# Forty-seven turns of the identity tile into unread PSUM tiles in the opening of a chunk-select attention and gated FFN kernel

## The chip, the cores and the metric

The kernel runs on one core of a Trainium2 chip. The metric is the device time of one execution in microseconds. Four compute engines work beside each other: TensorE (PE in the profile; its weight loads are PEld), VectorE (DVE), ScalarE (ACT) and GpSimd (POOL). SyncE (SP) issues most of the DMA transfers, GpSimd the ones for the weights. Each engine takes its instructions in the order of its own queue and waits for the others by semaphores.

## The reference

Attention over selected chunks comes first, for 4 batches, 8 heads, 768 positions and a head size of 64, and then a gated FFN over its 3072 rows of 512.

```python
k_chunks = k.reshape(B, H, nc, 32, D)                      # 24 chunks of 32 keys
k_min, k_max = k_chunks.min(3), k_chunks.max(3)
ub = sum over d of max(q * k_min, q * k_max)               # an upper bound per query and chunk
ub = where(chunk of the query >= chunk, ub, -1e9)
sel = the 6 chunks with the highest ub, per query
scores = where(sel and causal, q @ k.T / 8, -1e9)
x = softmax(scores) @ v                                    # -> [3072, 512]
out = (sigmoid(x @ w_gate) * (x @ w_val)) @ w_out          # d_ff = 1536
```

## The kernel before

The 3072 rows are cut into eight units of 384 rows (three blocks of 128). Unit 0 holds the first blocks of batches 0, 1 and 2, whose queries see fewer than six chunks, so nothing is selected for them; these blocks go through their own short path (`first`, L590). The other units take the remaining blocks in order. For each unit the kernel brings keys and queries into the layout with the head dimension on the partitions, works out the bounds and the selection (`choose`), attends, and runs the FFN. Units 4 to 7 run their FFN in pairs with sums of weights prepared beforehand.

Every operation is first written down as an entry of a plan (`Plan.add`, L50) with a name, the engines that it can run on, what it reads and what it writes. The durations that stand in the entries are not read when the kernel is built. The order of all operations is a list written out by hand, the string `ORDER` (L95): each word is an operation's name, behind `@` its engine if it isn't the first of its entry, and behind `:` the slots of the buffers that it is the first to use. PSUM tiles (`ps`) have eight slots, one per bank. `Plan.order` (L79) goes through the words, and each engine's queue holds its operations in that order. A tile that takes a slot waits for the last reader of the tile that had it before.

The names that matter in the opening, all of them in the list's first lines:

- `ident` (L461): `make_identity` on GpSimd fills `ident32`, a 128x128 float32 identity; `ident16` is its float16 copy.
- `kf{e}_{b}`, `qf{e}_{b}`, `vf_{b}` (L516 to L530): SyncE loads the first blocks' keys, queries and values of batch b. `k{p}_u1`, `q{p}_u1` and the same for u2 (L532) load keys and queries for units 1 and 2; `v_0_1` to `v_0_5` (L556) load the other value blocks of batch 0.
- `kfT_b`, `qfT_b` (L600): four float32 turns each on TensorE (`nc.tensor.transpose` with `ident32`) of the first blocks; `kf16_b`, `qf16_b` cast the results to float16.
- `scf_b` (L637): eight score matmuls; `expf` (L642) the exponential; `cmf` (L644) the causal mask on GpSimd; `pvf` (L651) the product with the values; `rzf`, `xf` the division on VectorE; `xpsf` (L666) two float16 turns of the result, `xTf` its copy to SBUF.
- `kn`, `kT`, `qn`, `qT` (L675 to L688): for units 1 and 2, a copy of the raw block and then three or two float32 turns on TensorE.
- `after0`, `after1` (L496): two one-element copies on GpSimd that read a landed query tile. The weights' loads `wg`, `wv`, `wo` (L501 to L510), three of each on GpSimd's DMA queue, depend on them.
- `g_u0_*`, `v_u0_*` (L937): the FFN of unit 0, and `o*_u0_*` (L968) its output product; `pv_u1_*` (L881) unit 1's product with the values; `v16_0_*` (L564) GpSimd's casts of the value blocks.

TensorE's queue in the opening is: `qfT_1`, `kT_u1_1`, `kfT_0`, `qfT_0`, `scf_0`, `kfT_1`, `kfT_2`, `scf_1`, `qfT_2`, `pvf_0_0`, `pvf_0_1`, `xpsf_0_0`, `pvf_1_0`, `xpsf_0_1`, `scf_2`, `xpsf_1_0`, `pvf_2_0`, `kT_u1_0`, and so on up to `g_u0_0`.

Of the kernel before, what the change touches and what calls it, by code (L numbers as in the profile page):

```python
# [99 lines left out]
expf_0_1:3 q1_u1 pvf_0_0:6 qf16_2:4 after1 rzf_0_0:0 k1_u2:1 cmf_0_1 xf_0_0:0 kt_u1_1:0 q1_u2 cmf_1_0 vc_1@ACT  # L100
pvf_0_1:7 k2_u2 xpsf_0_0:0,0 v11 expf_1_1:1 pvf_1_0:5 k3_u2 vc_2 rzf_1_0:0 rzf_0_1:1 hq1 cmf_1_1 xf_0_1:1 hkp101 wg1
kxf0 q0_u2 kxf1:0 xpsf_0_1:4 scf_2:6,3,3 expf_2_0 qn_u1_0@POOL:1 kn_u1_2:5 expf_2_1:2 xf_1_0:2 cmf_2_0 ap1 kn_u1_0:2
wv1 kx1_u1_1:1 xpsf_1_0:7 pvf_2_0:6 xTf_0_0@ACT kT_u1_0:2 xTf_0_1 cmf_2_1 rzf_2_0:0 xf_2_0:0 k0_u2 pvf_1_1:5 wg2
kx1_u1_0 xpsf_2_0:3 qn_u1_3:4 pvf_2_1:0 hk1_u1_1@ACT rzf_2_1:0 wv2 qn_u1_2@DVE:2 wo1 v_0_3:5 xf_2_1:1 rzf_1_1:0
xTf_2_0 qT_u1_0:1 xf_1_1:2 kn_u1_3:6 wo0 xTf_1_0 kT_u1_2:4 hkp110@ACT kt_u1_0@DVE:1 kx0_u1_0 qT_u1_3:6 v_0_2:3
hkf0@ACT qn_u1_1@POOL:0 qf_u1_3:0 xpsf_1_1:0 qf_u1_0 xpsf_2_1:3 xTf_2_1 kT_u1_3:5 xTf_1_1 qT_u1_2:7 qf_u1_2@DVE
g_u0_0:2,0,0 kx0_u1_3 hq0_u1_2@POOL qT_u1_1:3 kcr_f v_u0_0:0 qm_u1_2@POOL:0 qf_u1_1@DVE qm_u1_0@ACT g_u0_1:7,1,1
kx1_u1_2 hq0_u1_0 qm_u1_3@POOL kx1_u1_3 tanh_u0_0 v_u0_1:6 qm_u1_1@POOL kt_u1_2@DVE:2 g_u0_2:1,2,2 kx0_u1_2
hk1_u1_2@ACT vf1_3:1 kcr1 kcr_u1@POOL hk0_u1_2@ACT hg_u0_0 v_u0_2:3 ub_u1:2,4 tanh_u0_2 hk0_u1_0 tanh_u0_1 hg_u0_2
# [5 lines left out]
sc_u1_3_1:2,0 v_u0_7:4 hk0_u2_2@POOL kT_u2_0:3 exp_u1_0_2 sc_u1_3_2:6 hq1_u1_2@POOL g_u0_8:1,3,8 hq0_u2_1@DVE
hk1_u1_3@ACT hk1_u1_0@POOL exp_u1_1_2 kx1_u2_2:0 v_u0_8:7 qn_u2_0:0 ap1_u1 exp_u1_3_2 kx0_u2_2 sc_u1_3_0:0 sc_u1_2_2:6
apt1_u1 exp_u1_3_0 sc_u1_2_1:5 hg_u0_7 kn_u2_3:5 kf0_3 qT_u2_0:0 cm_u1_3 hqm1_u1_2@DVE exp_u1_2_2 sc_u1_0_0:4 cm_u1_1
qf_u2_0 g_u0_9:6,2,9 exp_u1_3_1 tanh_u0_8 kT_u2_1:0 hq0_u2_0@POOL v_u0_9:2 hq1_u1_1 cm_u1_2 kx1_u2_1 hqm1_u1_0@ACT
hg_u0_8 g_u0_10:1,1,10 kx0_u2_0 v_u0_10:7 exp_u1_2_1 kx1_u2_0 tanh_u0_10 hk1_u2_2 kT_u2_3:5 exp_u1_0_0 hg_u0_10
g_u0_11:1,0,11 kx1_u2_3 cm_u1_0 sc_u1_0_1:4 kt_u2_3@DVE:0 v_u0_11:7 hkf1 exp_u1_0_1 kx0_u2_3 tanh_u0_9 v16_0_3  # L120
o0_u0_0:4,0 kt_u2_0:2 hg_u0_9 tanh_u0_11 hk1_u2_3@POOL hk1_u2_0 kt_u2_1:1 sc_u1_1_1:5 q2_u2 o1_u0_0 hg_u0_11
hk0_u2_1@ACT q3_u2 kx0_u2_1 exp_u1_1_1 k11_1:0 hq1_u1_0 qf1_3:2 v16_0_2 o2_u0_0 v16_0_1 hk0_u2_3@POOL pv_u1_2:6
osb_u0_0@DVE kfT_3:3 qn_u2_3:4 sc_u1_5_0:2,2 kcr_u2 qn_u2_2:2 pv_u1_1:1 kf16_3@DVE:0 qf0_3 pv_u1_0 qT_u2_3:7 out_u0_0
rz_u1_0:0 qT_u2_2:0 sc_u1_6_2:5,3 pv_u1_3 k01_1 qf_u2_2 sc_u1_7_0:4,0 exp_u1_5_0 rz_u1_1:1 o0_u0_1:3,1 vf_3:1 qm_u2_2
qf_u2_3@DVE hq0_u2_2 x_u1_0:0 exp_u1_6_2 sc_u1_7_2:0 sc_u1_4_2:2,1 x_u1_1:2 exp_u1_7_2 sc_u1_7_1:7 o1_u0_1 exp_u1_4_2
qm_u2_3 exp_u1_7_0 qm_u2_0 sc_u1_5_2:1 hq1_u2_1 sc_u1_6_0:5 cm_u1_7 exp_u1_7_1 sc_u1_5_1:0 cm_u1_5 exp_u1_5_1
sc_u1_4_0:6 ub_u2:2,4 k10_1 exp_u1_6_0 k00_1 exp_u1_5_2 xps_u1_0:7,1 exp_u1_4_0 sc_u1_6_1:0 ubn0_u2:0 sc_u1_4_1:5
qfT_3:1 xT_u1_0 exp_u1_4_1 cm_u1_4 mx0_u2:0 o2_u0_1 hk0_u2_0@ACT hq0_u2_3@POOL ubn1_u2 exp_u1_6_1 hq1_u2_3@POOL
pv_u1_5:2 qf16_3:6 mx1_u2 cm_u1_6 pv_u1_7:6 vc_3@ACT pv_u1_4 v_0_5:5 hq1_u2_0@DVE pv_u1_6 rz_u1_2:0 scf_3:7,5,0 ap1_u2
# [1235 lines left out]
```

## Time and profile before

| | |
|---|---|
| Median of three runs | 289.07 us (287.99 to 289.54) |
| The profiled execution | 286.49 us |
| Its span, first to last instruction | 284.5 us |
| TensorE busy | 265.6 us, 93% |
| VectorE busy | 248.8 us, 87% |
| ScalarE busy | 209.5 us, 74% |
| GpSimd busy | 162.1 us, 57% |
| DMA | 34.28 MB in 130035 packets |

How to read the rows below. Times count from the first instruction of the profiled execution. A row of the stretches gives for each engine the busy time and the number of instructions, then the granted clock, the mean busy share of the 16 DMA engines (over 1 where packets overlap) and the bytes moved per time. A row of the timeline gives start, duration, engine, source line, operation, tiles written and read, shape and count; in brackets stands how long the engine had been idle before and what ended that. A piece of the chain is a start, a duration and who worked; the chain follows what ended last back to its cause. A row of one tile gives the shortest, median and longest duration of one instruction. The duration of a matmul reaches to the arrival of its result, so matmuls that follow each other overlap: the pace is the distance between starts.

### The profile page before, as it was taken

The page shows a single profiled execution, that of the slowest core. Times are in us where ns is not written, and L with a number is a line of the kernel's source. Part 1 is how long each engine was busy: PE and PEld are TensorE (multiplying, and loading weights), DVE is VectorE, ACT ScalarE, POOL GpSimd, SP SyncE. Part 2 cuts the span into 40 slices and gives each one's busy share as a digit, 9 for nine tenths or more (in the row PEclk, how much of TensorE's full clock was granted, in tenths as well). Part 3 has the DMA queues.
Part 4 walks back from the last instruction along what each step waited for, and adds up shares of the span by engine and source line. Part 5 has one row for each costly group of instructions (what it writes and reads, how often), then busy time and mean ns, then how long its engine had stood idle before and what let it go on. Part 6 is the DMA issues. An engine that isn't in the chain of part 4 may idle for free.

```text
span 284.5 us, 7266 instructions
## 1 busy us (share of the span) xinstructions
PE 265.6 (93%) x2668; PEld 180.9 (64%) x2668; DVE 248.8 (87%) x660; ACT 209.5 (74%) x457; POOL 162.1 (57%) x231
## 2 busy tenths in 40 slices
PE   1859999799999999999999999999899999999994
PEld 1637565567764666664767756676476786765784
DVE  6569987569998998989979899999999989999972
ACT  2477579488779788668799997899899647758621
POOL 7298634246257559569776866357848700076720
PEclk9999999999999999999999999999999999999999
DMA  7999999999999999919335013030000211001005
GB/s 169 254 214 219 213 197 206 197 186 221 186 181 215 188 247 210 175 30 216 80 75 140 6 30 81 37 69 13 16 14 17 64 40 75 2 37 76 1 2 221
DMA packets 130035, 34.28 MB, mean 120 GB/s; under 512 B 118096, under 2 KB 127056, under 8 KB 130000
## 3 DMA queue, kind: packets, MB, share of 16 engines
q1 hardware_dynamic: 125248, 29.11, 48.5%
q0 software_dynamic: 4752, 4.72, 9.9%
q8 instruction: 21, 0.34, 0.5%
q14 instruction: 14, 0.11, 0.1%
HBM read 30.67 MB, written 6.29 MB: 130 GB/s over the span
## 4 chain that ended last, share of the span: by engine, by line
PE 66%; DVE 11%; DMA 9%; SPq 4%; ACT 3%; POOL 3%; issue 2%; DVEq 0%; POOLq 0%; ACTq 0%
PE sc_u L848 9%; PE o_u L968 9%; PE g_u L937 8%; PE v_u L937 8%; PE pv_u L881 5%; DMA kq_u<-in_k_dram 5%; DMA v<-in_v_dram 4%; PE suo_u6u L1195 3%; PE suo_u4u L1195 2%; PE ube_u L787 2%; PE suv_u6u L1054 2%; DVE hg_u L1084 2%; PE sug_u6u L1054 2%; DVE hgp_u L1084 2%; SPq L538 2%
## 5 line engine op out<-in xcount | busy, mean ns | idle before, releaser
L859 ACT ACTIVATE att_u<-sc_u 128x512 f16<-128x512 f32 (+3 forms) x184 | 92.1, 552 | 15.9 <-PE sc_u L848 14.4
L865 POOL TENSOR_SCALAR_AFFINE_SELECT att_u<-att_u 128x384 f16<-128x384 f16 (+1 forms) x56 | 30.7, 556 | 44.3 <-ACT att_u L859 35.5
L937 PE MATMUL g_u<-xT_u,wg 128*128 128x384 f16 x192 | 39.1, 326 | 0.1
L937 PE MATMUL v_u<-xT_u,wv 128*128 128x384 f16 x192 | 39.0, 326 | 0.1
L968 PE MATMUL o_u<-wo,hg_u 128*128 128x512 f16 x144 | 35.3, 379 | 1.0 <-DMA wo<-in_moe_w_out_dram 1.0
L949 DVE SCALAR_TENSOR_TENSOR hg_u<-gate_u,v_u 128x384 f16<-128x384 f16 x48 | 25.1, 535 | 4.3 <-PE v_u L937 2.4
L881 PEld LDWEIGHTS <-att_u 128*128 128x128 f16 x640 | 24.9, 98 | 5.5 <-issue 1.5
L881 PE MATMUL pv_u<-v,att_u 128*128 128x65 f16 x640 | 27.3, 193 | 1.1 <-POOL v L564 1.0
L945 ACT ACTIVATE gate_u<-g_u 128x384 f16<-128x384 f32 x48 | 23.3, 495 | 6.7 <-PE g_u L937 6.5
L848 PE MATMUL sc_u<-hqe,hke 128*128 128x128 f16 (+2 forms) x220 | 27.8, 243 | 0.1
L848 PE MATMUL sc_u<-hqo,hko 128*128 128x128 f16 (+2 forms) x220 | 27.3, 243 | 0.1
L937 PEld LDWEIGHTS <-wg 128*128 128x128 f16 x192 | 18.1, 98 | 10.4 <-issue 0.8
L937 PEld LDWEIGHTS <-wv 128*128 128x128 f16 x192 | 18.1, 98 | 10.5 <-DMA wv<-in_moe_w_val_dram 0.4
L968 PEld LDWEIGHTS <-hg_u 128*128 128x128 f16 x144 | 13.2, 98 | 13.7 <-DVE kcr L572 1.3
L848 PEld LDWEIGHTS <-hke 128*128 128x128 f16 x220 | 17.0, 98 | 7.3 <-issue 1.0
L848 PEld LDWEIGHTS <-hko 128*128 128x128 f16 x220 | 16.8, 98 | 6.4 <-issue 0.9
L1177 POOL TENSOR_TENSOR v<-v,hg_u 128x384 f16<-128x384 f16 x6 | 6.0, 996 | 24.1 <-PE sug_u6u L1054 22.3
L564 POOL CAST v<-v 128x512 f16<-128x512 f32 x23 | 14.8, 644 | 7.0 <-DMA v<-in_v_dram 5.8
L900 DVE TENSOR_TENSOR x_u<-pv_u,rz_u 128x384 f16<-128x384 f32 (+1 forms) x28 | 14.7, 529 | 0.6
L1054 PEld LDWEIGHTS <-Sg 128*128 128x128 f16 x96 | 9.1, 98 | 6.1 <-issue 1.4
L810 DVE MAX8 mx_u<-ubn_u 128x8 f32<-128x8 f32 (+16 forms) x152 | 12.5, 158 | 0.3
L1054 PEld LDWEIGHTS <-Sv 128*128 128x128 f16 x96 | 9.0, 98 | 5.4 <-issue 0.5
(280 smaller groups left out, 699.3 us busy)
## 6 DMA issues: line engine op xcount, KB each, us to landing
...
wg<-in_moe_w_gate_dram POOLq DMA_DIRECT2D x3, 512.0 KB, 11.5
wv<-in_moe_w_val_dram POOLq DMA_DIRECT2D x3, 512.0 KB, 12.8
wo<-in_moe_w_out_dram POOLq DMA_DIRECT2D x3, 512.0 KB, 20.3
...
```

Source lines behind the costliest of these rows:

```text
L564: plan.add(f"v16_{b}_{ib}", {POOL: pool(H * D)}, lambda e: nc.gpsimd.tensor_copy(v16[b % 2][:, ib, :, 0:D], at(t)), reads=[t], writes=[("v ...
L848: nc.tensor.matmul(at(t)[:, o:o + 128 * m], hk[b % 2][e_][:, p, 128 * jb:128 * jb + 128], hq[u.side][e_][:, p, 128 * x:128 * (x + m)], sta ...
L859: plan.add(f"exp_{u.name}_{h}_{y}", {ACT: act(n)}, lambda e, t=t, att=att, b0=b0, n=n: nc.scalar.activation(at(att)[:, b0:b0 + n], at(t), ...
L865: nc.gpsimd.affine_select(out=dv, in_=dv, compare_op=ALU.is_ge, fill=0.0, base=0, pattern=[[0, u.m], [1, 128]], channel_multiplier=-1)
L881: nc.tensor.matmul(at(pv)[:, last, x, :], at(att)[:, c:c + 128], v16[b % 2][:, jb, h, :], start=(jb == 0), stop=(jb == ib))
L900: plan.add(f"x_{u.name}_{p}", {DVE: dve(u.t)}, lambda e: nc.vector.tensor_tensor(at(x_).rearrange("p a (e d) -> p e a d", e=2), at(pv)[:, ...
L937: nc.tensor.matmul(at(t), w16[:, c, 128 * fb:128 * fb + 128], at(u.xt)[:, c, :], start=(c == 0), stop=(c == 3))
L945: plan.add(f"tanh_{u.name}_{fb}", {ACT: act(T)}, lambda e, g=g, gate=gate: nc.scalar.activation(at(gate), at(g), AF.Tanh, scale=0.5), read ...
L949: plan.add(f"hg_{u.name}_{fb}", {DVE: dve(T)}, lambda e, w_=w_, gate=gate, hg=hg: nc.vector.scalar_tensor_tensor(at(hg), at(gate), 1.0, at ...
L968: nc.tensor.matmul(at(o), hgs[c][1][1]()[:, 128 * tb:128 * tb + 128], wo16[:, fc, lo:hi], start=(c == 0), stop=(c == NFB - 1))
L1054: nc.tensor.matmul(at(t), left[i](c), right[i](c), start=first and c == 0, stop=c == 1, skip_group_check=not first)
L1195: nc.tensor.matmul(at(t), sums[what[i][0], f][1]()[:, 128 * tb:128 * tb + 128], what[i][1](f), start=first and f == 0, stop=f == half - 1, ...
```

## The change

Seven operations, `beat0` to `beat6`, are added to the plan, and their names are put into the order. Each turns the identity tile by itself into a PSUM tile of its own, 19, 2, 4, 5, 2, 6 and 9 times, and nothing reads these tiles.

```diff
+BEATS = (19, 2, 4, 5, 2, 6, 9)
...
     const("ident", {POOL: (560, 600)}, lambda e: make_identity(nc, ident32), writes=["ident32"], prio=-20)
+    for i, n in enumerate(BEATS):
+        beat = ps(f"beat{i}", "pr", [128, 128])
+
+        def beats(e, n=n, beat=beat):
+            for _ in range(n):
+                nc.tensor.transpose(at(beat), ident32, ident32)
+
+        const(f"beat{i}", {PE: (213 * n, 213 * n + 170)}, beats, reads=["ident32"], writes=[beat])
```

The string `ORDER` is wrapped anew, so that all of its lines differ, but its words are the same except for seven that are inserted (the neighbours shown are the ones before and after each in the list):

```
 ... qf1_0 kf1_2:3 qf1_2:4          beat0:7   qfT_1:0 after0 kf0_1:5 ...
 ... kn_u1_1@DVE:2 kf0_2 hkp010     beat1:7   kT_u1_1:1 kf1_1 q0_u1 ...
 ... kf16_0@DVE:3 qf16_0@DVE:4 vf_2:1   beat2:7   scf_0:4,5,1 vf_1:2 ...
 ... q1_u2 cmf_1_0 vc_1@ACT         beat3:7   pvf_0_1:7 k2_u2 ...
 ... xpsf_0_0:0,0 v11 expf_1_1:1    beat4:5   pvf_1_0:5 k3_u2 ...
 ... kxf0 q0_u2 kxf1:0              beat5:4   xpsf_0_1:4 scf_2:6,3,3 ...
 ... kn_u1_0:2 wv1 kx1_u1_1:1       beat6:7   xpsf_1_0:7 pvf_2_0:6 ...
```

On TensorE's queue `beat0` is the first work and waits only for the identity; `beat1` stands between `qfT_1` and `kT_u1_1`, `beat2` between `qfT_0` and `scf_0`, and the other four ahead of `pvf_0_1`, `pvf_1_0`, `xpsf_0_1` and `xpsf_1_0`. The queues of the other engines and of the DMA hold the same operations in the same order as before.

More of the change, by code (lines that the diff above doesn't have):

```diff
@@ L100 @@
[L100 to L109, printed above, removed]
@@ L115 @@
[L115 to L124, printed above, removed]
@@ L125 @@
[L125 to L129, printed above, removed]
@@ L280 @@
-Q4_u6u7_0 F2_u6u7_0 out_u7_0 Q4_u6u7_2 F2_u6u7_2 out0_u7_2
+beat0:7 qfT_1:0 after0 kf0_1:5 hkp111 vf1_2:0 qf0_2 hkp001 v10 qf16_1:1 k0_u1 kn_u1_1@DVE:2 kf0_2 hkp010 beat1:7
+kT_u1_1:1 kf1_1 q0_u1 kfT_0:2 vf_0:0 qfT_0:3 k2_u1 kf16_0@DVE:3 qf16_0@DVE:4 vf_2:1 beat2:7 scf_0:4,5,1 vf_1:2 kfT_1:6
+expf_0_0 hkp000@ACT q2_u1 cmf_0_0 kf16_1@DVE:5 kfT_2:7 vf1_1:6 wg0 kcr0 scf_1:0,3,2 kx0_u1_1 kf16_2:2 q3_u1 v16_0_0
+qfT_2:4 expf_1_0 k3_u1 wv0 expf_0_1:3 q1_u1 pvf_0_0:6 qf16_2:4 after1 rzf_0_0:0 k1_u2:1 cmf_0_1 xf_0_0:0 kt_u1_1:0
@@ new lines @@
+q1_u2 cmf_1_0 vc_1@ACT beat3:7 pvf_0_1:7 k2_u2 xpsf_0_0:0,0 v11 expf_1_1:1 beat4:5 pvf_1_0:5 k3_u2 vc_2 rzf_1_0:0
+rzf_0_1:1 hq1 cmf_1_1 xf_0_1:1 hkp101 wg1 kxf0 q0_u2 kxf1:0 beat5:4 xpsf_0_1:4 scf_2:6,3,3 expf_2_0 qn_u1_0@POOL:1
+kn_u1_2:5 expf_2_1:2 xf_1_0:2 cmf_2_0 ap1 kn_u1_0:2 wv1 kx1_u1_1:1 beat6:7 xpsf_1_0:7 pvf_2_0:6 xTf_0_0@ACT kT_u1_0:2
+xTf_0_1 cmf_2_1 rzf_2_0:0 xf_2_0:0 k0_u2 pvf_1_1:5 wg2 kx1_u1_0 xpsf_2_0:3 qn_u1_3:4 pvf_2_1:0 hk1_u1_1@ACT rzf_2_1:0
+wv2 qn_u1_2@DVE:2 wo1 v_0_3:5 xf_2_1:1 rzf_1_1:0 xTf_2_0 qT_u1_0:1 xf_1_1:2 kn_u1_3:6 wo0 xTf_1_0 kT_u1_2:4 hkp110@ACT
@@ new lines @@
+kt_u1_0@DVE:1 kx0_u1_0 qT_u1_3:6 v_0_2:3 hkf0@ACT qn_u1_1@POOL:0 qf_u1_3:0 xpsf_1_1:0 qf_u1_0 xpsf_2_1:3 xTf_2_1
+kT_u1_3:5 xTf_1_1 qT_u1_2:7 qf_u1_2@DVE g_u0_0:2,0,0 kx0_u1_3 hq0_u1_2@POOL qT_u1_1:3 kcr_f v_u0_0:0 qm_u1_2@POOL:0
+qf_u1_1@DVE qm_u1_0@ACT g_u0_1:7,1,1 kx1_u1_2 hq0_u1_0 qm_u1_3@POOL kx1_u1_3 tanh_u0_0 v_u0_1:6 qm_u1_1@POOL
+kt_u1_2@DVE:2 g_u0_2:1,2,2 kx0_u1_2 hk1_u1_2@ACT vf1_3:1 kcr1 kcr_u1@POOL hk0_u1_2@ACT hg_u0_0 v_u0_2:3 ub_u1:2,4
+tanh_u0_2 hk0_u1_0 tanh_u0_1 hg_u0_2 kt_u1_3:2 qn_u2_1@DVE:5 kn_u2_2@POOL:4 hg_u0_1 g_u0_3:0,3,3 hq1_u1_3@POOL
@@ new lines @@
+hq1_u1_2@POOL g_u0_8:1,3,8 hq0_u2_1@DVE hk1_u1_3@ACT hk1_u1_0@POOL exp_u1_1_2 kx1_u2_2:0 v_u0_8:7 qn_u2_0:0 ap1_u1
+exp_u1_3_2 kx0_u2_2 sc_u1_3_0:0 sc_u1_2_2:6 apt1_u1 exp_u1_3_0 sc_u1_2_1:5 hg_u0_7 kn_u2_3:5 kf0_3 qT_u2_0:0 cm_u1_3
+hqm1_u1_2@DVE exp_u1_2_2 sc_u1_0_0:4 cm_u1_1 qf_u2_0 g_u0_9:6,2,9 exp_u1_3_1 tanh_u0_8 kT_u2_1:0 hq0_u2_0@POOL
+v_u0_9:2 hq1_u1_1 cm_u1_2 kx1_u2_1 hqm1_u1_0@ACT hg_u0_8 g_u0_10:1,1,10 kx0_u2_0 v_u0_10:7 exp_u1_2_1 kx1_u2_0
+tanh_u0_10 hk1_u2_2 kT_u2_3:5 exp_u1_0_0 hg_u0_10 g_u0_11:1,0,11 kx1_u2_3 cm_u1_0 sc_u1_0_1:4 kt_u2_3@DVE:0 v_u0_11:7
@@ new lines @@
+hkf1 exp_u1_0_1 kx0_u2_3 tanh_u0_9 v16_0_3 o0_u0_0:4,0 kt_u2_0:2 hg_u0_9 tanh_u0_11 hk1_u2_3@POOL hk1_u2_0 kt_u2_1:1
+sc_u1_1_1:5 q2_u2 o1_u0_0 hg_u0_11 hk0_u2_1@ACT q3_u2 kx0_u2_1 exp_u1_1_1 k11_1:0 hq1_u1_0 qf1_3:2 v16_0_2 o2_u0_0
+v16_0_1 hk0_u2_3@POOL pv_u1_2:6 osb_u0_0@DVE kfT_3:3 qn_u2_3:4 sc_u1_5_0:2,2 kcr_u2 qn_u2_2:2 pv_u1_1:1 kf16_3@DVE:0
+qf0_3 pv_u1_0 qT_u2_3:7 out_u0_0 rz_u1_0:0 qT_u2_2:0 sc_u1_6_2:5,3 pv_u1_3 k01_1 qf_u2_2 sc_u1_7_0:4,0 exp_u1_5_0
+rz_u1_1:1 o0_u0_1:3,1 vf_3:1 qm_u2_2 qf_u2_3@DVE hq0_u2_2 x_u1_0:0 exp_u1_6_2 sc_u1_7_2:0 sc_u1_4_2:2,1 x_u1_1:2
@@ new lines @@
+exp_u1_7_2 sc_u1_7_1:7 o1_u0_1 exp_u1_4_2 qm_u2_3 exp_u1_7_0 qm_u2_0 sc_u1_5_2:1 hq1_u2_1 sc_u1_6_0:5 cm_u1_7
+exp_u1_7_1 sc_u1_5_1:0 cm_u1_5 exp_u1_5_1 sc_u1_4_0:6 ub_u2:2,4 k10_1 exp_u1_6_0 k00_1 exp_u1_5_2 xps_u1_0:7,1
+exp_u1_4_0 sc_u1_6_1:0 ubn0_u2:0 sc_u1_4_1:5 qfT_3:1 xT_u1_0 exp_u1_4_1 cm_u1_4 mx0_u2:0 o2_u0_1 hk0_u2_0@ACT
+hq0_u2_3@POOL ubn1_u2 exp_u1_6_1 hq1_u2_3@POOL pv_u1_5:2 qf16_3:6 mx1_u2 cm_u1_6 pv_u1_7:6 vc_3@ACT pv_u1_4 v_0_5:5
+hq1_u2_0@DVE pv_u1_6 rz_u1_2:0 scf_3:7,5,0 ap1_u2 o0_u0_2:4,0 apt1_u2:0 expf_3_0 ap0_u2 expf_3_1:2 rz_u1_3:1 x_u1_2:1
@@ new lines @@
+sc_u4_5_0:0 exp_u4_5_0 sc_u4_6_2:4 sc_u4_4_3:3 hk0_3_3@DVE exp_u4_4_3 ap1_u5 g_u3_3:6,3,14 tanh_u3_3 qf0_u7_1:1
+k16_3_2:6 cm_u4_0 hk1_2_2 sc_u4_6_3:2 exp_u4_6_3 sc_u4_6_0:7 exp_u4_6_0 hqm0_u5_2 pv_u4_0 v_u3_3:3 qm_u6_2@POOL:0
+qf1_u6_1 sc_u4_4_0:2 exp_u4_4_0 kx1_3_1 kx0_3_2 qf0_u7_2 sc_u4_4_1:7 exp_u4_4_1 sc_u4_7_0:6,1 sc_u4_5_1:0
+g_u3_4:1,2,15 v_u3_4:7 g_u3_5:2,1,2 cm_u4_6 exp_u4_6_2 pv_u4_6:4 hg_u3_3 tanh_u3_4 hg_u3_4 v_u3_5:7 g_u3_6:3,2,16
+v_u3_6:1 hq0_u6_0@ACT tanh_u3_5 exp_u4_7_0 exp_u4_5_1 hg_u3_5 tanh_u3_6 qm_u6_0@ACT g_u3_7:0,1,17 tanh_u3_7 cm_u4_4
@@ new lines @@
+hqm0_u5_0 v_3_1:2 sc_u5_3_0:3,0 exp_u5_3_0 sc_u4_7_1:7 sc_u4_7_2:6 exp_u4_7_2 hq1_u6_0@POOL cm_u4_5 pv_u4_5:2 hk0_3_1
+v16_2_4 sc_u5_1_0:0,2 exp_u5_1_0 qf0_u7_3 rz_u4_0:0 x_u4_0:1 qf0_u7_0 exp_u4_7_1 hg_u3_6 kt_3_2:5 pv_u4_4 rz_u4_2:0
+x_u4_2:2 Sv0:1 xT_u4_0 out_u2_1 xT_u4_2 v_2_5:5 apt1_u5 v_u3_7:3 hg_u3_7 sc_u5_1_2:0 exp_u5_1_2 sc_u4_7_3:6 exp_u4_7_3
+hk1_3_0@ACT Sg2:0 hk0_3_2@DVE g_u3_8:1,2,1 v_u3_8:7 hk1_3_1 tanh_u3_8 hg_u3_8 sc_u5_0_0:6,3 sc_u5_3_1:0 sc_u5_0_2:2
+g_u3_9:3,1,3 tanh_u3_9 hk0_3_0@DVE kcr_3@POOL ub_u6:1,5 ubn0_u6:0 ubm0_u6 cm_u5_1 cm_u4_7 pv_u4_7 hq0_u6_2@POOL
@@ new lines @@
+exp_u5_5_1 hq0_u7_2@POOL pv_u5_2 rz_u5_1:1 hg_u3_11 x_u5_1:0 hg_u3_9 sc_u5_5_0:0 exp_u5_5_0 Sv1 sc_u5_4_0:7,1
+exp_u5_4_0 o0_u3_0:6,0 cm_u5_4 apt0_u6 sc_u5_7_1:0 exp_u5_7_1 sc_u5_7_0:5 exp_u5_7_0 ub_u7:7,1 ubn0_u7:0 v16_3_2
+ubn1_u7 mx1_u7:0 mx0_u7 cm_u5_5 hqm0_u6_2@DVE Sg0 hqm1_u6_0@ACT sc_u5_6_2:5 exp_u5_6_2 sc_u5_4_1:0 exp_u5_4_1
+sc_u5_5_2:3 exp_u5_5_2 sc_u5_6_1:4 sc_u5_4_2:7 exp_u5_6_1 exp_u5_4_2 o1_u3_0 o2_u3_0 osb_u3_0 v16_2_5 pv_u5_5:4
+hqm0_u6_0 cm_u5_7 xT_u5_0:1 sc_u6_1_1:7,3 sc_u6_1_0:3 exp_u6_1_0 cm_u6_1 hk1_3_2 pv_u5_7:0 sc_u6_0_0:6,2 exp_u6_0_0
@@ new lines @@
+tanh_u4u5_1_0:1 hg_u4u5_1_0 v16_3_4 hqm0_u7_0 hq1_u6_2@POOL xT_u6_0:0 sc_u6_7_0:3,2 exp_u6_7_0 P4g_u4u5_0
+tanh_u4u5_0_6:1 P7g_u4u5_1 C3g_u4u5_1 v_3_3:4 sc_u6_7_2:1 exp_u6_7_2 tanh_u4u5_1_6:2 cm_u6_2 pv_u6_2 rz_u6_1:0
+x_u6_1:2 xT_u6_1 P7v_u4u5_0 C3v_u4u5_0 v16_3_5 sc_u6_6_0:4,1 exp_u6_6_0 tanh_u4u5_1_1:1 cm_u6_5 pv_u6_5:1 cm_u6_4
+pv_u6_4 rz_u6_2:0 P2g_u4u5_1 C0g_u4u5_1 sc_u7_1_1:4,0 exp_u7_1_1 x_u6_2:0 xT_u6_2 P4g_u4u5_1 tanh_u4u5_0_7:0
+sc_u7_1_0:7 exp_u7_1_0 P1v_u4u5_1:0,3,5 E0v_u4u5_1@DVE:2 P4v_u4u5_0 hg_u4u5_0_6 P2v_u4u5_1 C0v_u4u5_1 tanh_u4u5_0_1:3
@@ new lines @@
+exp_u7_2_3 P1v_u4u5_3:5,4,6 hg_u4u5_1_8 P3g_u4u5_3 C1g_u4u5_3 P4v_u4u5_2 E0v_u4u5_3:3 P2v_u4u5_3 C0v_u4u5_3
+tanh_u4u5_1_2:1 hg_u4u5_1_2 tanh_u4u5_0_3:3 sc_u7_3_1:7 exp_u7_3_1 P7g_u4u5_3 P6v_u4u5_3 E1v_u4u5_3:4
+P1g_u4u5_4:4,2,3,0,12,3 E0g_u4u5_4:0 P5g_u4u5_4 C3g_u4u5_3 hg_u4u5_0_8 P5v_u4u5_3 E3v_u4u5_3:6 E3g_u4u5_4:1 P2g_u4u5_4
+C0g_u4u5_4 hg_u4u5_0_3 So0 cm_u7_0 P7v_u4u5_3 C3v_u4u5_3 sc_u7_2_1:1 exp_u7_2_1 P4g_u4u5_3 tanh_u4u5_0_9:2
+S1_u4u5_2@POOL tanh_u4u5_1_9:0 sc_u7_2_2:2 exp_u7_2_2 P6g_u4u5_4 E1g_u4u5_4@DVE:5 P3g_u4u5_4 C1g_u4u5_4 pv_u7_0:0
```

288 lines of the change are left out of this document (130 added, 158 removed).

## The prediction

> **What bounds the kernel now.** I read the page first, then busy time by stretches, then the chain of waits, then TensorE's timeline up to 53 us.
>
> ```profile
> span 284.5 us, 7266 instructions
> PE 265.6 (93%) x2668; PEld 180.9 (64%) x2668; DVE 248.8 (87%) x660; ACT 209.5 (74%) x457; POOL 162.1 (57%) x231
> PEclk9999999999999999999999999999999999999999
> ```
>
> TensorE is busy 93% of the span, so 18.9 us of it are idle. The stretches say where:
>
> ```profile
> core 0: us, PE busy (x) PEld busy (x) DVE busy (x) ACT busy (x) POOL busy (x), PEclk, DMA share, GB/s
> 0.00:24.03 24.03, 13.49 (x94) 10.83 (x95) 15.55 (x35) 11.18 (x20) 16.44 (x32) 1.00 0.99 214
> 24.03:48.00 23.97, 23.56 (x183) 14.38 (x182) 21.25 (x75) 18.07 (x42) 13.10 (x23) 1.00 1.21 206
> 48.00:52.28 4.28, 2.31 (x13) 0.97 (x11) 2.39 (x6) 1.75 (x5) 1.71 (x5) 1.00 0.77 179
> 52.28:80.00 27.72, 27.62 (x327) 19.39 (x327) 22.88 (x62) 21.88 (x51) 10.38 (x19) 1.00 1.06 195
> ```
>
> There are 10.5 us of idle time before 24 us, almost none from there to 48, then 2.0 us at once between 48 and 52.28, and from 52.28 on TensorE is dense (27.62 of 27.72). The DMA engines are full from the first loads to 48 us (share 0.99 with 2 us of start in it, then 1.21). The reader should keep one picture: an opening limited by loads, one last wait at 52 us, and then some 230 us limited by TensorE.
>
> The chain's pieces that end late in the opening, and TensorE's rows for its last wait:
>
> ```profile
> 10.92 0.60 PE scf L637 x7
> ...
> 17.77 13.40 DMA kq_u<-in_k_dram
> ...
> 39.32 12.24 DMA v<-in_v_dram
> 51.61 0.63 POOL v L564
> ```
>
> ```profile
> 50.23 1.02 PE L968 MATMUL o_u<-wo,hg_u 128*128 128x512 f16 x4 [0.98 <-DMA wo<-in_moe_w_out_dram]
> ...
> 52.28 0.40 PE L881 MATMUL pv_u<-v,att_u 128*128 128x65 f16 x8 [0.99 <-POOL v L564]
> ```
>
> Both waits end on a landing: first wo, then a value block issued at 39.32 that took 12.24 us to land behind everything queued before it. TensorE, ScalarE and VectorE all stood idle there (2.31, 1.75 and 2.39 busy of 4.28), so nobody was late but the load.
>
> **The clock before 24 us.** The granted clock reads 9 tenths or more everywhere, but the durations contradict it for the first 24 us, and I go by durations:
>
> ```profile
> 8.23 1.06 PE L600 MATMUL kfT<-ident,kf 128*128 128x128 f32 x4
> ...
> 23.76 0.62 PE L686 MATMUL qT_u<-ident,qn_u 128*128 128x128 f32 x3
> ...
> 24.65 0.50 PE L686 MATMUL kT_u<-ident,kn_u 128*128 128x128 f32 x3
> ```
>
> ```profile
> L600 PE MATMUL kfT<-ident,kf x16: 272/421/472, 8.2 to 52.9; 128*128 128x128 f32 x16
> ```
>
> One float32 turn lasts 0.42 us early and 0.27 late. Four of them in 1.06 us start (1.06 - 0.42) / 3 = 0.213 us apart; three of them in 0.50 us start (0.50 - 0.272) / 2 = 0.114 us apart. So TensorE runs at about half pace until the row at 23.76 and at full pace after it. What came before the rise, and what didn't bring it:
>
> ```profile
> 10.92:15.24 4.32, 4.31 (x32) 3.36 (x31) 1.52 (x3) 3.65 (x6) 3.03 (x6) 1.00 1.07 253
> 15.24:20.32 5.08, 1.93 (x21) 1.15 (x21) 3.52 (x11) 3.16 (x7) 4.52 (x9) 1.00 1.13 210
> 20.32:24.00 3.68, 3.53 (x27) 3.26 (x28) 3.31 (x12) 2.47 (x7) 3.67 (x7) 1.00 1.19 228
> ```
>
> A busy stretch of 3.7 us ended in full pace, and one of 4.3 us did not: length alone does not decide it.
>
> **The change part by part.** Nothing is removed, and no other operation changes place on any engine. Added are 47 float32 turns of ident32, in seven groups of 19, 2, 4, 5, 2, 6 and 9. At slow pace they take 47 x 0.213 = 10.0 us of TensorE, at full pace 47 x 0.114 = 5.4. Here is what they are to lie in:
>
> ```profile
> 1.07 0.29 POOL masks.py:199 TENSOR_SCALAR_AFFINE_SELECT ident<-ident 128x128 f32<-128x128 f32 x1
> ```
>
> ```profile
> 5.79 1.08 PE L600 MATMUL qfT<-ident,qf 128*128 128x128 f32 x4 [5.79 <-POOL hke L357]
> 7.53 0.90 PE L686 MATMUL kT_u<-ident,kn_u 128*128 128x128 f32 x3 [0.66 <-DVE kn_u L355]
> 10.92 0.61 PE L637 MATMUL scf<-qf,kf 64*128 64x128 f16 x8 [0.78 <-DVE qf L355]
> 16.00 0.40 PE L651 MATMUL pvf<-v,attf 128*128 128x65 f16 x4 [0.76 <-POOL attf L644]
> 16.92 0.38 PE L651 MATMUL pvf<-vf,attf 128*128 128x65 f16 x4 [0.31 <-ACT vf L353]
> 18.10 0.40 PE L666 MATMUL xpsf<-ident,xf 128*128 128x128 f16 x2 [0.80 <-DVE xf L659]
> 20.32 0.39 PE L666 MATMUL xpsf<-ident,xf 128*128 128x128 f16 x2 [1.28 <-DVE xf L659]
> ```
>
> Group 1: the identity is there at 1.36; 19 x 0.213 = 4.05 us puts its end near 5.5, before 5.79, so it costs nothing. Were that cover gone, qfT would be late by what sticks out. Groups 2 to 7, slow pace against the wait: 0.43 in 0.66; 0.85 in 0.78; 1.07 in 0.76; 0.43 in 0.31; 1.28 in 0.80; 1.92 in 1.28. At slow pace 0.07 + 0.31 + 0.12 + 0.48 + 0.64 = 1.62 us stick out; at full pace (0.23, 0.46, 0.57, 0.23, 0.68, 1.03) all fit. Each group writes a PSUM bank that is free there or that the next operation takes anyway, so its own waits are ones that stood there already, and nothing reads what it writes.
>
> When does the pace rise? With group 1, TensorE works without a gap from about 1.4 to 5.5, and with group 3 the stretch from 7.53 has no gap up to 15.24. The bounds: at about 5.1, if the first 3.7 us do it as they did before 24; at the other end not before 24. I take between 7 and 12, nearer the early rows, since two stretches longer than 3.7 us now lie there, one of them nearly 8 us.
>
> What the rise brings at best. The 11 turns from 7.53 to scf shrink by 11 x (0.213 - 0.114) = 1.1 us, but VectorE's two casts are behind them in series:
>
> ```profile
> 9.33 0.69 DVE L355 CAST kf<-kfT 128x512 f16<-128x512 f32 x1 [1.39 <-PE kfT L600]
> 10.18 0.69 DVE L355 CAST qf<-qfT 128x512 f16<-128x512 f32 x1 [0.16 <-PE qfT L600]
> ```
>
> The first waits for seven turns and their tail (0.84 less, at 8.5), the second ends at 9.9, so scf starts at 9.95 in place of 10.92: 0.95 us. In the stretch from 20.32, 3.53 us of slow work shrink to 3.53 x 0.114 / 0.213 = 1.9, 1.64 us less. Together TensorE can stand up to 2.6 us further on at 25 us. With the late bound it is 0 to 1.6 us behind instead.
>
> What becomes of those 2.6 us. They run into the wait at 48 to 52.28, whose end is a landing. SyncE's loads keep their order and the DMA engines are full, so a transfer that is issued sooner only stands longer in line. The room left in the engines while TensorE was slow is what can be won:
>
> ```profile
> 9.00:10.00 1.00, 1.00 (x6) 0.74 (x4) 0.67 (x1) 0.00 (x0) 0.00 (x0) 1.00 0.93 222
> 15.00:16.00 1.00, 0.24 (x6) 0.08 (x3) 0.60 (x2) 1.00 (x3) 1.00 (x4) 1.00 0.96 202
> ```
>
> That is 0.07 + 0.04 = 0.1 us. So the sum is: 284.5 us of span, -0.1 for the landing, 0 for 47 beats inside waits, 0 for the faster start (it makes 2.0 us of idle time into at most 4.6). 284.4 us of span and the 2.0 us around it (the profiled execution took 286.49) make 286.4. That execution is 0.9% under the median of the runs shown, 289.07; the same step from 289.07 gives 289.0.
>
> Against the change speaks a rule of the Trainium skill, "TensorE: Matmul & The Clock Gate", Part 4: a transpose on TensorE does not bring the full clock, since it does not count as busy in the same way. By that, the beats would never raise the pace. The trace disagrees in part: the turns themselves nearly double their pace at 23.76, and no row shows whether they brought it about. By the rule the sum would be 290.4, worked out below as the third rival; by the rows it is the one above.
>
> **The rivals.**
>
> First, the gain passes through: the landing at 51.6 hangs on how early TensorE frees buffers and releases issues, not on full engines. For it: scf at 10.92 is a piece of the chain, ahead of the loads. Against it: the share of 1.21 for 24 us. It would give up to 0.95 + 1.64 = 2.6 us: 286.5.
>
> Second, an earlier start of the weights starves the keys:
>
> ```profile
> 12.84 1.00 POOL L503 DMA_DIRECT2D wg<-in_moe_w_gate_dram  x1
> wg<-in_moe_w_gate_dram POOLq DMA_DIRECT2D x3, 512.0 KB, 11.5
> ```
>
> This issue waits behind the mask that scf feeds. Nine such loads between 12.84 and wo's landing at 50.23 are 4.7 MB in 37.4 us, 126 of 206 GB/s. A start 0.95 us sooner takes 0.12 MB from the other loads, which get 80 GB/s: 1.5 us later for the keys in the chain, which land at 17.77 + 13.40 = 31.17 now. The 2.0 us at 48 cover that too; if TensorE is not ahead by then, a remainder of about 0.5: 289.6.
>
> Third, slower: the beats stay at slow pace, as if turns raised nothing. Then 1.62 us stick out, all in waits with TensorE's own work behind them, and the rise at 24 comes one stretch of 3.68 us later, which loses 3.68 x (1 - 0.114 / 0.213) = 1.7 more. Of 3.3 us the wait at 48 covers 2.0: 1.3 are left, 290.4. It decides from 2.0 us of delay on. For it: 4.3 dense us without a rise. Against it: float32 turns of keys and queries are a part of the 3.53 busy us ahead of the rise, and matmuls alone did not fill that stretch.
>
> That the pace rises and falls again in the waits from 15.24 to 20.32 (TensorE busy 1.93 of 5.08) is a rival to the deed, not to the time: it lies between forecast and third rival, inside the cover.
>
> **How the numbers follow.** A measurement of this kernel can tell about 0.5% (1.45 us) from no change: 287.6 to 290.5. Forecast, hidden at the landing, 289.0: 0.62. Gain passes through, 286.5, more or less of it: 0.22. Weights ahead of keys, 289.6: 0.06. Slow beats, 290.4: 0.10. Faster takes the second figure and a little of the forecast's scatter (the runs shown span 287.99 to 289.54): 0.25. Slower takes about half of the last, some of the third figure and the scatter: 0.13. Same: 0.62. The range runs from the first rival to the third, 286.6 to 290.5.
>
> **What would show it.** Right: turns from 8 to 15 us closer to 0.114 than to 0.213 apart, scf near 10, more idle time than 2.0 us between 46 and 53 with the value block still landing at 51 to 52, and the same dense work after it. Wrong: pv_u's wait ends 1 us or more sooner (first rival), the turns at 12 us still 0.213 apart (third), the keys for u2 landing after 32.5 (second). The forecast fails if the landing moves with TensorE, or if something after 52.28 that I took for fixed changes its length.

## The result, and the profile after

| | before | after |
|---|---|---|
| Median of 20 runs each | 288.12 us (285.78 to 289.54) | 291.57 us (287.69 to 294.42) |
| Ratio after / before, 95% interval | | 1.0082 (1.0053 to 1.0111) |
| The profiled execution, and its span | 286.49, 284.5 us | 293.74, 292.0 us |
| First weights issued (`wg0`) | 12.84 | 11.60 |
| Cast of batch 1's values (`vf`) on ScalarE | 16.25 | 24.85 |
| First FFN matmul (`g_u0_0`) | 25.54 | 35.02 |

The change makes the kernel 0.8% slower, where 289.0 us, no change, was forecast, and 291.57 lies above the range. The ratio leaves out the longest runs, which is why it is smaller than the 3.4 us between the medians; the profiled execution of after is itself one of the longer ones, so the 7.5 us that its span has over the one of before show where the time goes, and more of it than is usual.

The page of after, its first lines and the line of the granted clock:

```profile
span 292.0 us, 7361 instructions
PE 270.5 (93%) x2715; PEld 185.6 (64%) x2715; DVE 248.7 (85%) x660; ACT 209.6 (72%) x457; POOL 161.6 (55%) x231
PEclk9975899999999999999999999999999999999999
```

TensorE is busy 4.9 us longer (47 more instructions), and idle 21.5 us where it was 18.9. The clock is granted at half for a while in slices 3 to 5, that is between 15 and 37 us. Busy time by stretches of after (PE, PEld, DVE, ACT, POOL with their counts, then the granted clock, the DMA share and GB/s):

```profile
15.00:20.00 5.00, 1.08 (x13) 0.70 (x11) 0.51 (x2) 0.45 (x2) 2.26 (x6) 0.76 1.06 179
20.00:24.03 4.03, 0.00 (x0) 0.00 (x0) 0.00 (x0) 0.00 (x0) 0.00 (x0) 0.50 1.17 249
24.03:48.00 23.97, 21.49 (x179) 15.05 (x179) 20.54 (x72) 14.19 (x30) 14.20 (x22) 0.85 1.18 217
48.00:52.28 4.28, 3.98 (x31) 2.55 (x30) 2.97 (x14) 4.21 (x12) 2.47 (x6) 1.00 1.42 216
```

From 20 to 24 us no engine does anything while the DMA engines are full. In exchange the wait at 48 to 52.28 is nearly gone: TensorE is busy 3.98 of 4.28 us there, against 2.31 before. TensorE's timeline of after tells what it stood waiting for:

```profile
1.41 4.32 PE L469 MATMUL beat<-ident 128*128 128x128 f32 x19 [1.41 <-POOL ident masks.py:199]
...
7.52 0.55 PE L696 MATMUL kT_u<-ident,kn_u 128*128 128x128 f32 x3
...
9.89 0.40 PE L647 MATMUL scf<-qf,kf 64*128 64x128 f16 x8 [0.51 <-DVE qf L357]
...
25.52 0.38 PE L661 MATMUL pvf<-vf,attf 128*128 128x65 f16 x4 [8.84 <-ACT vf L355]
25.71 1.52 PE L469 MATMUL beat<-ident 128*128 128x128 f32 x6
28.14 2.18 PE L469 MATMUL beat<-ident 128*128 128x128 f32 x9
35.02 0.88 PE L947 MATMUL g_u<-xT_u,wg 128*128 128x384 f16 x4
```

The row `pvf<-vf,attf` is `pvf_1_0`; before, it stood at 16.92 after a wait of 0.31. Now it waits 8.84 us for ScalarE's cast of `vf`, and that cast waits for a landing. The three rows behind this, from GpSimd's, ScalarE's and SyncE's timelines of after:

```profile
11.60 0.99 POOL L513 DMA_DIRECT2D wg<-in_moe_w_gate_dram  x1
24.85 0.62 ACT L355 CAST vf<-vf 128x512 f16<-128x512 f32 x1 [9.41 <-DMA vf<-in_v_dram]
10.82 2.34 SPq L532 DMA_DIRECT2D vf<-in_v_dram  x2
```

The same of before, ScalarE's and SyncE's (GpSimd's stands in the prediction):

```profile
16.25 0.62 ACT L353 CAST vf<-vf 128x512 f16<-128x512 f32 x1 [0.15 <-DMA vf<-in_v_dram]
10.30 2.22 SPq L522 DMA_DIRECT2D vf<-in_v_dram  x2
```

And the view of the tile `vf` up to 40 us, the time from issue to landing of its loads, first of before, then of after:

```profile
DMA to landing us min/median/max: 4.2/4.4/5.4
```

```profile
DMA to landing us min/median/max: 4.5/4.5/13.5
```

The chain of waits of after has the same load as its longest piece, and behind it the beats:

```profile
11.33 13.49 DMA vf<-in_v_dram
24.85 0.63 ACT vf L355
25.90 1.35 PE beat L469 x6
27.66 0.54 PE scf L647 x8
28.21 1.09 PE beat L469 x5
```

So the books close for the profiled executions: `g_u0_0` starts 9.5 us later (35.02 against 25.54), the wait at 48 to 52 had 2.0 us to give, and 7.5 us remain, which is the difference of the spans. What is left open by the two traces is why one load of 256 KB took 13.5 us, and how much of the loss is the beats' own work behind it.

### The profile page after: what moved, and what is told of

It reads as the page before. It is cut to its first block, busy times and chain, and to the rows that moved or that the text cites. A ratio compares the mean times of both kernels' runs of the same rounds, so it can differ in the third digit from the quotient of the medians.

```text
span 292.0 us, 7361 instructions
## 1 busy us (share of the span) xinstructions
PE 270.5 (93%) x2715; PEld 185.6 (64%) x2715; DVE 248.7 (85%) x660; ACT 209.6 (72%) x457; POOL 161.6 (55%) x231
## 3 DMA queue, kind: packets, MB, share of 16 engines
q1 hardware_dynamic: 125248, 29.11, 47.1%
q0 software_dynamic: 4752, 4.72, 9.9%
## 4 chain that ended last, share of the span: by engine, by line
PE 72%; DVE 10%; DMA 6%; ACT 5%; SPq 2%; issue 2%; POOL 1%; DVEq 0%; ACTq 0%
PE g_u L947 11%; PE v_u L947 10%; PE sc_u L858 10%; PE o_u L978 10%; PE pv_u L891 5%; DMA vf<-in_v_dram 5%; PE suo_u6u L1205 3%; PE ube_u L797 3%; PE suo_u4u L1205 2%; PE suv_u6u L1064 2%; ACT att_u L869 2%; PE sug_u6u L1064 2%; SPq L537 2%; DVE hgp_u L1094 2%; DVE hg_u L1094 2%
## 5 line engine op out<-in xcount | busy, mean ns | idle before, releaser
L654 POOL TENSOR_SCALAR_AFFINE_SELECT attf<-attf 128x512 f16<-128x512 f16 x8 | 5.0, 633 | 15.8 <-ACT attf L652 15.8
L764 DVE STREAM_TRANSPOSE qf_u<-q 128x384 f32<-128x384 f32 (+2 forms) x28 | 11.8, 438 | 1.3 <-DMA q<-in_q_dram 1.3
```

## The experiments

Three theories stood at the start. Q, the queue: the early clock brings scf, and with it the first weights' issue, 1.24 us forward; the weights then share the DMA engines with the values' loads still in line and make these late. B: beats stand in the way as work. C: the clock, which falls to half in the long wait, costs the time afterwards.

**Beats kept, the weights held where they were.** A copy of about 1 us on GpSimd (into the place of `wo`, which is loaded later) stands ahead of `wg0`.

```diff
-... vf1_1:6 wg0 kcr0 scf_1:0,3,2 ...
+... vf1_1:6 fill0 wg0 kcr0 scf_1:0,3,2 ...
...
+    plan.add("fill0", {POOL: (1000, 1000)}, lambda e: nc.gpsimd.tensor_copy(
+        wo16[:, 0:2, :].rearrange("p a (b c) -> p (a b) c", c=128), ident32.unsqueeze(1).to_broadcast([128, 8, 128])),
+        reads=["ident32"], writes=[("wo", 0)])
```

> The changed kernel with one copy of about 1 us put on GpSimd's queue ahead of the first weights' load, so that this load goes out near 12.8 us, as in the kernel before, and not at 11.6. Theory Q (the earlier weights share the DMA engines packet for packet with the small value packets of vf, which then land 8 us late): vf lands near 16.5 us again, TensorE's 8.8 us wait is gone, and the time is 287.0 to 288.6 (ratio 0.996 to 1.002). Theory B (the beats themselves stand in the way of TensorE's work): still 290.5 to 292. Theory C (the clock, raised early, falls back in the following waits and stays at half pace for 13 us): the wait may shrink, but the half pace from 17 to 31 us stays, 290 to 291.

Measured: 288.18 us, ratio 0.9986 (0.9946 to 1.0027). GpSimd's, ScalarE's and TensorE's rows:

```profile
12.59 0.99 POOL L513 DMA_DIRECT2D wg<-in_moe_w_gate_dram  x1
16.34 0.62 ACT L355 CAST vf<-vf 128x512 f16<-128x512 f32 x1 [1.26 <-DMA vf<-in_v_dram]
25.61 0.81 PE L947 MATMUL g_u<-xT_u,wg 128*128 128x384 f16 x4
```

With all 47 beats in place and the weights issued at 12.59, the cast of `vf` is back at 16.34 and `g_u0_0` at 25.61, both within 0.1 us of before, and the loss is gone. The work of the beats alone costs nothing that these runs can tell from noise (about 0.4%).

**The weights early, no beats.** `wg0` moves ahead of the mask `cmf_0_0`; a one-element copy ties it to the landing of batch 1's keys in the first version, to batch 0's `qf16` cast in the second.

```diff
-cmf_0_0 kf16_1@DVE:5 kfT_2:7 vf1_1:6 wg0 kcr0 ...
+afterx wg0 cmf_0_0 kf16_1@DVE:5 kfT_2:7 vf1_1:6 kcr0 ...
...
-    weights(0, -0.9, ["after0"])
+    plan.add("afterx", {POOL: (110, 150)}, lambda e: nc.gpsimd.tensor_copy(word[0:1, 0:1], at(raw_f[1]["k"])[0:1, 1, 0:1]),
+             reads=[(raw_f[1]["k"], 1)], writes=["afterx"])
+    weights(0, -0.9, ["after0", "afterx"])
```

> The kernel before, without beats; only the first weights' load is put ahead of the first mask on GpSimd and tied to the landing of a key tile at about 11.4 us, so that it goes out some 1.3 us sooner than before. Theory Q: vf lands several us later than 16.3 (beyond 20), TensorE waits for it, and the time is 290 to 293 (ratio 1.006 to 1.017) with no beat in the program. Theories B and C: 287.5 to 288.7, nothing to see.

Measured: 288.62 us, 1.0008 (0.9975 to 1.0041), a miss of Q's number. The issue moved by only 0.54 us, to 12.30, and the cast of `vf` by 3.9:

```profile
12.30 0.99 POOL L503 DMA_DIRECT2D wg<-in_moe_w_gate_dram  x1 [0.37 <-issue]
20.15 0.62 ACT L353 CAST vf<-vf 128x512 f16<-128x512 f32 x1 [3.85 <-DMA vf<-in_v_dram]
```

The mechanism shows in the profiled execution (span 287.7), but half the dose doesn't move the median. In the second version, `afterx` reads the cast query tile:

```diff
+            if n == "q" and b == 0:
+                plan.add("afterx", {POOL: (110, 150)}, lambda e, h=half[n]: nc.gpsimd.tensor_copy(word[0:1, 0:1], at(h)[0:1, 0, 0:1]),
+                         reads=[half[n]], writes=["afterx"])
```

> The kernel before, without beats; the first weights' load is put ahead of the first mask on GpSimd and tied to the first query cast, so that it goes out near 11.0 us, 1.8 us sooner than before (the run before this one reached only 0.5 us). Theory Q: vf lands beyond 22 us, TensorE waits some 6 us or more for it, more than the 2 us that the later wait covers, and the time is 290 to 293 (ratio 1.006 to 1.017) at slow clock and with no beat. Theory B (beats in the way): 287.5 to 289.

Measured: 290.02 us, 1.0053 (1.0017 to 1.0090).

```profile
11.55 0.99 POOL L503 DMA_DIRECT2D wg<-in_moe_w_gate_dram  x1 [0.38 <-issue]
21.93 0.62 ACT L353 CAST vf<-vf 128x512 f16<-128x512 f32 x1 [5.46 <-DMA vf<-in_v_dram]
22.60 0.38 PE L654 MATMUL pvf<-vf,attf 128*128 128x65 f16 x4 [5.74 <-ACT vf L353]
```

Without a single beat, an issue at 11.55 makes the same kind of wait of TensorE (5.74 us, 8.84 in the profiled execution of after) and a slower kernel. With the first experiment this shows that the weights' issue is what costs: it is enough alone, and without it no cost of the beats is seen.

**Half of the beats.** First only the three front groups, which raise the clock, are kept; then only the last four, which lie in the waits behind.

```diff
     for i, n in enumerate(BEATS):
+        if i not in (0, 1, 2):
+            continue
```

> The changed kernel with the last four groups of turns (5, 2, 6 and 9) left out; the first three (19, 2 and 4) stay. Theory Q: scf and the first weights are as early as in the changed kernel, vf lands late, 290 to 292. Theory B: the turns at half pace that stood in the chain at 25.9 and 28.2 us (1.35 and 1.1 us) are gone, 288.5 to 289.5. Theory C: 290.5 to 292, since nothing holds the clock in the waits.

Measured: 291.3 us (four runs), 1.0128 (1.0084 to 1.0171); `wg0` at 11.61, `g_u0_0` at 31.52, and this wait of TensorE in the view of waits (total, times, longest):

```profile
PE pvf L663 <- ACT vf L355: 5.9, 1, 5.9
```

```diff
     for i, n in enumerate(BEATS):
+        if i not in (3, 4, 5, 6):
+            continue
```

> Only the last four groups of turns (5, 2, 6 and 9) are kept, the first three are left out, so the clock does not rise early and scf and the first weights go out as in the kernel before. Theory Q: 287.5 to 289 (ratio 0.998 to 1.003); the turns at half pace push TensorE by up to 1.6 us at 20 us, which the wait at 48 to 52 takes up. Theory B: 289.5 to 291.

Measured: 287.15 us, 0.9981 (0.9944 to 1.0017); `wg0` at 12.83. ScalarE's row:

```profile
17.26 0.62 ACT L354 CAST vf<-vf 128x512 f16<-128x512 f32 x1 [0.77 <-DMA vf<-in_v_dram]
```

The three front groups carry the whole loss, the 22 turns behind them none. From the cast of `vf` to `g_u0_0` it takes 9.57 us without the last four groups (21.95 to 31.52), 10.17 with them (24.85 to 35.02) and 9.29 before. Between the two executions the 2.4 us of beats that stand in the chain of after cost about 0.6 us, and all that after has over before in this stretch is 0.9.

**The weights later than before.** `wg0` behind `v16_0_0`, in the kernel after and in the one before.

```diff
-... vf1_1:6 wg0 kcr0 scf_1:0,3,2 kx0_u1_1 kf16_2:2 q3_u1 v16_0_0 ...
+... vf1_1:6 kcr0 scf_1:0,3,2 kx0_u1_1 kf16_2:2 q3_u1 v16_0_0 wg0 ...
```

> The changed kernel with the first weights' load moved behind the cast of the first value block on GpSimd's queue (it then goes out at about 14.4 us). Theory Q: vf lands by 16.5 us; the head start of the beats is kept and the time is 286.5 to 288.5. Theory B: 290.5 to 292. Theory C: 289.5 to 291.

> The kernel before, without beats, with the first weights' load moved behind the cast of the first value block (from 12.8 to about 14.4 us). Theory Q with its other side: vf is safe, but all weights are 1 to 1.5 us later and TensorE waits for wv or wo instead: 288.3 to 289.8, as the same swap did with beats (289.1). If the early start of the weights costs nothing here, 287 to 288.

Measured: 289.12 us, 1.0031 (0.9993 to 1.0068), with beats; 288.76 us, 1.0030 (1.0001 to 1.0058), without. `wg0` goes out at 13.94 and 13.98, and the cast of `vf` starts at 15.67 and 15.94, sooner than before. If the weights were now the late ones, the views of waits of the two, with and without beats, would show it at wo:

```profile
PE o_u L978 <- DMA wo<-in_moe_w_out_dram: 0.9, 2, 0.7
```

```profile
PE o_u L968 <- DMA wo<-in_moe_w_out_dram: 1.0, 1, 1.0
```

They don't: the second line is word for word that of before, where TensorE waited 1.0 us for wo too, and only with beats is there a new wait for wv, of 0.5 us. In these two executions `g_u0_0` starts at 25.47 and 25.75, against 25.54 before, so that the 2.4 and 1.7 us that their spans (286.9 and 286.2) have over the one of before lie behind it, by a cause that stays open. Q's number for the first was missed: taking the loss away this way doesn't leave a gain. For the second it was met, but not by the wait that Q named. Moving `wg0` in either direction brought no gain.

**A smaller dose.** As the first experiment, but with a copy of about 0.6 us (`wo16[:, 0:1, :]`, four tiles in place of eight).

> The changed kernel with a copy of about 0.6 us ahead of the first weights' load, so that it goes out near 12.1 to 12.2 us, half way between the changed kernel (11.6) and the one before (12.8). Theory Q: vf lands between 17 and 22 us, and the time lies between that of hold12 and that of the changed kernel, 288.5 to 290.5. If only something else about the copy had healed hold12, it is 291 or more.

Measured: 288.93 us, 1.0052 (1.0019 to 1.0085), with `wg0` at 12.16. Q's number was met, the landing that it named only at the edge: the profiled execution (287.55, one of its shortest) has the cast of `vf` at 16.97, so it doesn't show where the others lose. It isn't typical of them: its mean granted clock is 0.992, so that it was at half pace for (1 - 0.992) x 2 x 285.8 = 4.6 us; the other eleven have 0.980 to 0.988, or 7 to 12 us.

**The values ahead in SyncE's line.** `vf_2` and `vf_1` move ahead of `k2_u1`, first in after, then in before, then in after with the copy of 1 us.

```diff
-kT_u1_1:1 kf1_1 q0_u1 kfT_0:2 vf_0:0 qfT_0:3 k2_u1 kf16_0@DVE:3 qf16_0@DVE:4 vf_2:1 beat2:7 scf_0:4,5,1 vf_1:2 kfT_1:6
+kT_u1_1:1 kf1_1 q0_u1 kfT_0:2 vf_0:0 qfT_0:3 vf_2:1 vf_1:2 k2_u1 kf16_0@DVE:3 qf16_0@DVE:4  beat2:7 scf_0:4,5,1  kfT_1:6
```

> The changed kernel with the two value loads vf of batches 1 and 2 moved one place ahead on SyncE's queue, before a key load of unit 1. Theory Q: the value packets are mostly through when the weights' packets begin; vf lands by 19 us in place of 24.8, and the time is 287.5 to 289.5. Theory B: as the changed kernel, 290.5 to 292.

> The kernel before, without beats, with the two value loads vf of batches 1 and 2 one place ahead on SyncE's queue. Theory Q: the runs of before in which vf comes late lose less, 286.5 to 288 (ratio 0.994 to 1.0). If the key load that now comes later was as urgent, 288.5 to 289.5.

> The changed kernel with the copy of 1 us ahead of the first weights' load and the two value loads moved ahead: early clock, weights at their old time, values safe. Theory Q: 286.5 to 288 (ratio 0.994 to 1.0); the early clock itself brings nothing beyond 1 us, since the loads of keys and queries for unit 1 and the later wait at 48 to 52 us set the pace.

Measured, in this order: 289.07 us, 1.0025 (0.9988 to 1.0063); 288.39 us, 1.0021 (0.9989 to 1.0054); 288.68 us, 1.0035 (1.0003 to 1.0067). ScalarE's row of the first:

```profile
18.82 0.62 ACT L355 CAST vf<-vf 128x512 f16<-128x512 f32 x1 [1.95 <-DMA vf<-in_v_dram]
```

With the weights still at 11.61, value loads that go out about 1 us sooner (all three from 9.32 on) bring a cast that is late by 2.6 us in place of 8.6, which agrees with Q. Q's range for the second and the third, 286.5 to 288, was missed by both. In the third, with the weights held too, `vf` is cast at 15.76, but `g_u0_0` comes at 28.25: something else is late, by its view of waits the copies of unit 1's keys and queries, whose loads had moved back.

```profile
PE kT_u L696 <- ACT kn_u L355: 2.1, 2, 1.3
PE qT_u L696 <- ACT qn_u L355: 1.6, 1, 1.6
```

Here are the profiled executions in a table, with the distance from SyncE's issue of the last two value loads (`vf_2`, `vf_1`) to the issue of `wg0`:

| kernel | vf issue | wg0 issue | between | vf cast | ratio |
|---|---|---|---|---|---|
| before | 10.30 | 12.84 | 2.54 | 16.25 | 1 |
| last four groups | 10.36 | 12.83 | 2.47 | 17.26 | 0.9981 |
| beats, copy of 1 us | 10.15 | 12.59 | 2.44 | 16.34 | 0.9986 |
| no beats, tied to keys | 10.49 | 12.30 | 1.81 | 20.15 | 1.0008 |
| beats, copy of 0.6 us | 10.55 | 12.16 | 1.61 | 16.97 | 1.0052 |
| three front groups | 10.40 | 11.61 | 1.21 | 21.95 | 1.0128 |
| no beats, tied to qf16 | 10.45 | 11.55 | 1.10 | 21.93 | 1.0053 |
| after | 10.82 | 11.60 | 0.78 | 24.85 | 1.0082 |

On the whole, the smaller the distance, the later the values; the copy of 0.6 us doesn't fit. This would also say why after's profiled execution is worse than that of the three front groups with the weights at the same time: SyncE's issues happened to be 0.4 us later in it. The order was read from the traces afterwards, from one execution each, and wasn't forecast.

None of these kernels is faster than before beyond its interval.

## Why the prediction was wrong

*The clock* was right. The turns of `kT_u` at 7.52 are (0.55 - 0.27) / 2 = 0.14 us apart, and the granted clock's records put the rise at 7.37, inside "between 7 and 12"; scf starts at 9.89, forecast 9.95. The third rival, beats at slow pace, falls with it. So does, for this kernel, the rule of the Trainium skill that was weighed against the change ("TensorE: Matmul & The Clock Gate", Part 4): nothing but float32 turns had run on TensorE when the clock rose. That the rise lies inside "between 7 and 12" is partly luck: in the six other kernels with the same three front groups it came at 4.84, 5.09, 5.60, 6.23, 6.49 and 7.31, with scf at 9.89 or 9.90 in all of them. What the prediction left open, why a busy stretch of 4.3 us did not raise the pace and one of 3.7 did, is taken up in the last section.

*Group 1* was right within 0.2 us: its 19 turns end at 5.73, and qfT starts at 6.00, not 5.79, after 0.27 us of waiting for its queries.

*The cover at 48 to 52.28* was right: it was there, and 2.0 us of delay disappeared in it.

*What becomes of the 2.6 us* is the step that failed: "SyncE's loads keep their order and the DMA engines are full, so a transfer that is issued sooner only stands longer in line", priced at 0, and with it the second rival, which saw the weights' earlier issue and priced it by bytes: 0.12 MB, 1.5 us later, covered, 289.6 with a chance of 0.06. The mechanism of the second rival is what happened, but the price and the victim were wrong. The victim is not the keys for u2 but the values of batch 1, for whose landing ScalarE and, through its cast, TensorE already waited before (0.15 and 0.31 us), so that they had no slack at all: their cast came 8.6 us later in after, and 5.7 in the kernel without beats (tied to qf16). And the queues don't share by bytes. The page of before (queue, packets, MB, share of 16 engines) had the price:

```profile
q1 hardware_dynamic: 125248, 29.11, 48.5%
q0 software_dynamic: 4752, 4.72, 9.9%
```

A load's packet of SyncE's queue q1 has 29.11 MB / 125248 = 232 bytes on the average and takes 0.485 x 284.5 x 16 / 125248 = 17.6 ns of one engine; a packet of the weights' queue q0 has 993 bytes and takes 0.099 x 284.5 x 16 / 4752 = 94.8 ns. If an engine takes them in turn, a load's packet costs 112 ns while weights are in line. A 256 KB load of values, in rows of 64 float32, is 1024 packets of 256 bytes, 64 an engine: 1.1 us alone, 7.2 in turn. On top of the undisturbed 4.5 that is, as an estimate, 4.5 + 6.1 = 10.6 us to the landing. Measured were 10.6 (no beats, tied to qf16), 10.1 (three front groups) and 13.5 (after). Counts of packets that ended in a stretch of 2 us, weights' queue / SyncE's queue, from the records of the traces:

```
             14-16       16-18       18-20
before       38 / 1062   304 / 93
after       145 / 281    233 / 363   203 / 708
copy 1 us    98 / 1155   390 / 5
             26-28       30-32       40-42
before      283 / 282    299 / 295   310 / 310
```

In the stretches in which both queues have work for the whole 2 us, like those of before from 26 us on, the counts are equal to within 2%, and 16 engines x 2 us / 283 is 113 ns for a packet of each, the price above. In after the weights begin early enough to take SyncE's queue from about 1060 packets in 2 us to 281, while the values stand in it; before, the values were through. The Trainium skill has the rule ("DMA: Bandwidth & Descriptors", section "Queues, rings and completion order"): an engine goes round its queues packet by packet. From 26 us of before on the counts agree (283 and 282). While the weights set in, SyncE's queue got less than its turn: from 15 to 17 us of after the records hold 225 packets of weights and 24 of SyncE's. Why, they don't show; so the match of the estimate with 10.6 and 10.1 is partly luck, and the 3 us that after has over it are not explained.

*The first rival*, that the gain passes through, isn't seen in the times even where the weights were held: with the copy of 1 us, scf stays early, `g_u0_0` is at 25.61 and the ratio 0.9986 (0.9946 to 1.0027). On that point the forecast was right that the early clock alone brings no gain that can be told. Its trace does have the sign that the prediction named for this rival: the wait for the value block ends at 50.91 against 52.28, 1.4 us sooner where 0.1 was allowed, in one execution whose span is 0.8 us shorter.

*Theory C*, the fallen clock, isn't settled, but its part is small: after's clock is at half from 17.61 to 31.27, but the kernel without beats (tied to qf16), whose three float32 turns still take 0.85 us at 29.43 and 0.50 from 30.37 on, so that it runs at half pace about as long, has the same distance from the cast of `vf` to `g_u0_0` (21.93 to 31.21, 9.28) as before (9.29), which ran its opening at half pace up to 24.03 as well. At most the 0.9 us by which after's 10.17 exceeds before's 9.29 can be laid to it and the beats together, in one execution.

Open: how much the lateness of `vf` varies from run to run (after's runs go from 287.69 to 294.42, with one trace among them), and what keeps the kernels with the weights or the values moved from gaining. The granted clocks of after's runs give a hint at the first: the two at 0.988 took 288.4 us on average, the eleven at 0.981 or 0.982 took 291.3, the six at 0.974 to 0.977, the profiled one among them, 292.6, and the one at 0.970 took 293.8. That is some 7, 10, 14 and 17 us at half pace. If the time at half pace goes with the wait for `vf`, most runs waited less than the profiled one; no trace shows it. On the second, a part lies far behind the opening: TensorE waits 1.4 us for VectorE at 141 us in after with the values ahead, and 1.5 us at 142 with the weights later, where before has no such wait.
